# Pooled attention and a gated convolution: two blocks convolved at once without exchanged copies of h, and keys loaded and pooled by pairs of sequences

## The chip, the cores and the metric

The kernel runs on one core of a Trainium2 chip. The metric is device time in microseconds (us). The core has five engines that work side by side, each through its own queue of instructions in order: TensorE (matrix products and transposes, PE in the profile; its weight loads are listed apart as PEld), VectorE (DVE), ScalarE (ACT), GpSimd (POOL) and SyncE (SP). Data move between main memory and the on-chip memory (SBUF) by DMA; here GpSimd issues nearly all loads and SyncE nearly all stores. TensorE writes its results into eight PSUM banks, from which VectorE or ScalarE fetch them. An instruction waits until the semaphores of the work it depends on are set, and everything behind it on its engine waits with it.

## The reference

Eight sequences of 576 rows, eight heads of 64 columns. Keys and values are averaged over 8 rows each, so that 72 are left per head; the queries attend to these; the result, with the heads beside each other (512 columns), goes through a feed-forward part with a convolution of three taps along the sequence, which forms a gate.

```python
k_p = k.reshape(B, H, Sp, pool, D).mean(axis=3)      # B=8, H=8, Sp=72, pool=8, D=64
v_p = v.reshape(B, H, Sp, pool, D).mean(axis=3)
scores = scale * np.matmul(q, k_p.transpose(0, 1, 3, 2))
attn = np.exp(scores - np.max(scores, axis=-1, keepdims=True))
attn = attn / (np.sum(attn, axis=-1, keepdims=True) + 1e-09)
x = np.matmul(attn, v_p)          # then (B, S, H * D): 8 x 576 x 512
h = np.maximum(x @ w_in, 0.0)     # 512 -> 1024
conv_out = sum(conv_w[t][None, None, :] * hp[:, t:t + S, :] for t in range(3))   # hp: h, padded by a row
gate = 1.0 / (1.0 + np.exp(-conv_out))
out = h * gate @ w_out            # 1024 -> 512, float32
```

## The kernel before

**Order.** Every piece of work is an `Op` with a key (`Graph`, L34). `Graph.order` (L97) plays the program through with assumed durations and buffers and, whenever an engine comes free, takes the ready piece with the smallest key (TensorE prefers, by `STAY`, a piece of the array mode it is in). The order that this gives is the order of each engine's queue on the chip; the durations in it only choose that order. The constants (`STAY` to `URGENT`) and the table `NUDGE` (L70) shift the keys of kinds of work and of single pieces: ('l', ...) are the loads at the start, ('k', b), ('q', b), ('v', b) the preparation of a sequence, ('a', b) its attention, ('f', b) its feed-forward part, ('o', b) its output product. On-chip buffers come in rings (L300); a piece that takes a buffer waits until the last user of the one before is through. PSUM is given out by banks or pairs of neighbouring banks (`place`, L139).

**Groups.** The eight sequences go in four groups of two. A group has nine attention tiles of 128 rows (`parts`, L548): t 0 to 3 of its first sequence, t 4 half of each (the split tile), t 5 to 8 of its second; 36 in all.

**Loads and keys.** GpSimd issues the loads, which turn float32 into bfloat16 on the way. A key or query load (`load_heads`, L352) puts 576 rows of 64 for each of eight heads into four heaps of 128 partitions, 9 rows on each. Keys of sequence 0 come in two halves, queries of sequence 0 in two parts. `prep_k` (L464) pools and turns the keys on TensorE, by products with a pooling matrix `pm`; in the mode HALF these are 36 products of 144 columns on half the array, in QUARTER 72 of 72 columns on a quarter. `copy_k` (L487) brings them to `kT`. `prep_q` (L526) turns queries by transposes; `copy_q` copies them. `prep_v` (L499) sums values on VectorE in three adds (L503: 1280, 640, 320 columns) and multiplies them by a mask of heads into `vm` (L507, 960 columns; its `mask` operand is read with a step of 0 along the 64 columns).

**Attention tile.** Scores (L572 or L585), maximum on VectorE (`negm`, L598), shift on VectorE (`sd`, L610) or, in group 0, TensorE (L618), exponential on ScalarE (L636), its transpose to `eT` by TensorE and a copy (L661) in groups 0 and 1 and by a DMA of SyncE (L656) in groups 2 and 3, product with the values (L672), reciprocal and division on VectorE (L685, L687, `x<-psum,r`: "the division"), and a transpose to `xT`, by TensorE (L704) for groups 0 and 1, by a DMA (L696) after.

**Feed-forward part.** For each of the eight blocks `fb` of 128 columns of h: the input product (`ffn_in`, L717, 8 matmuls of 288 columns) and relu on ScalarE (L726). Sequence 0 has it by tiles of rows (L738, L748). The convolution (`ffn_conv`, matmuls at L803) multiplies by diagonal 64x64 matrices `dw`, one for each tap, on the four quarters of the array: two halves r of the input partitions times two halves c of the output's. Half r of the columns (288 of 576) is given to input half r, so each output half c needs both, and for r unequal to c the rows of h have to lie in the other half of the partitions. `ffn_swap` (copies at L783) makes these exchanged copies `hX`, two of 64x1152 for each pair of blocks, on VectorE or ScalarE:

```python
for n in range(max(map(len, todo))):
    for r in range(2):
        for c in range(2):
            ...
                out=cps[c * D:(c + 1) * D, r, lo:hi],
                lhsT=dw[r * D:(r + 1) * D, int(r != c), tap * n_fb + fb, :],
                rhs=hT[r * D:(r + 1) * D, fb, src:src + hi - lo] if r == c
                else hX[r * D:(r + 1) * D, fb % 2, src:src + hi - lo],
```

ScalarE takes tanh of half the sum (L815), VectorE adds 1 (L825) and multiplies by h (L826) into `gT`: "the gate". The output product (`ffn_out`, L833, eight matmuls of 512 columns a tile) needs all eight gates of the sequence, for the split tile those of both; it is copied from PSUM by VectorE or ScalarE (L844) and stored (`ffn_store`, L856) by two DMAs of 64 rows from SyncE. The last tile alone is copied in two halves of columns by both engines, and its two stores go from SyncE and from ScalarE (L1130 to L1136).

**Pieces that the change touches.** `add_load` (L904), `add_prep` (L972, keys and queries), `add_prep_v` (L1006), `add_ffn` (L1069) and `early` (L921, the loads of the start).

## Time and profile before

| | |
|---|---|
| median of 3 runs | 244.5 us (244.48 to 244.52) |
| profiled execution, span | 244.0 us |
| mean granted TensorE clock in it | 0.996 |
| TensorE busy | 220.9 us, 91% of the span |
| VectorE busy | 182.0 us, 75% |
| ScalarE busy | 168.3 us, 69% |
| GpSimd busy | 29.1 us, 12% |
| read from / written to main memory | 32.52 / 9.44 MB |

The profile is of one execution, whose span of 244.0 us runs from the first to the last instruction. Durations of instructions, and times counted from the span's start, are from it. A matmul's end is modelled and matmuls overlap, so TensorE's busy time is not a measure of how near it is to its full pace. A row of a group of instructions gives: line of the kernel, engine, operation, output<-inputs, shapes, count | busy us, mean ns of one | idle time of the engine just before them and what ended most of it. The row of busy shares in 40 slices has a digit for each 6.1 us, in tenths. Rows of a stretch begin with from:to and its length in us, then for PE, PEld, DVE, ACT, POOL the busy us and the number of instructions, the granted clock, the DMA share and GB/s. Rows of the timeline begin with the time and the duration; "ACTq" and "SPq" there are the instructions by which those engines issue a DMA.

### The profile page before, as it was taken

How to read it: one execution, taken by the hardware profiler on the slowest of the kernel's cores; microseconds unless marked ns; L12 is line 12 of the kernel's file. 1: busy time of each engine (PE TensorE's matmuls, PEld its weight loads, DVE VectorE, ACT ScalarE, POOL GpSimd, SP SyncE). 2: the span in 40 equal slices, each digit the busy share in tenths (PEclk: the TensorE clock that was granted, in tenths of full speed). 3: DMA queues.
4: the chain of work that ended last, by engine and by line, in shares of the span. 5: the costliest groups of instructions: out<-in, count | busy, mean ns of one | idle time of the engine just before them, and what ended most of it. 6: DMA issues, size and time to landing. Idle time of an engine off the chain costs nothing.

```text
span 244.0 us, 7852 instructions
## 1 busy us (share of the span) xinstructions
PE 220.9 (91%) x3354; PEld 154.3 (63%) x3377; DVE 182.0 (75%) x398; ACT 168.3 (69%) x264; POOL 29.1 (12%) x48
## 2 busy tenths in 40 slices
PE   6568998998999999999999996979999999899991
PEld 2446986876675676678775554757655576676440
DVE  7667648899999999999999995755799413956301
ACT  2254764599996876498998654949966386989330
POOL 7942223200122020220010000000000000000000
PEclk9999999999999999999999999999999999999998
DMA  5999999999189958697208568593216577400356
GB/s 81 164 205 207 207 208 208 207 207 202 22 141 185 197 83 190 104 179 153 46 3 141 126 134 91 107 139 89 24 46 149 109 137 167 117 3 6 84 137 164
DMA packets 43707, 31.53 MB, mean 129 GB/s; under 512 B 23680, under 2 KB 39064, under 8 KB 43672
## 3 DMA queue, kind: packets, MB, share of 16 engines
q0 software_dynamic: 15952, 16.26, 42.2%
q1 hardware_dynamic: 27640, 14.64, 29.5%
q8 instruction: 26, 0.43, 0.7%
q10 hardware_dynamic: 80, 0.13, 0.2%
q14 instruction: 9, 0.07, 0.1%
HBM read 32.52 MB, written 9.44 MB: 172 GB/s over the span
## 4 chain that ended last, share of the span: by engine, by line
PE 51%; DVE 26%; ACT 8%; DMA 7%; issue 5%; POOL 0%; SPq 0%; DVEq 0%; ACTq 0%; POOLq 0%
PE psum L833 16%; PE psum L717 14%; PE psum L803 7%; DVE negm L598 5%; DVE gT L826 4%; PE psum L672 3%; DVE sd L610 3%; DMA kp<-in_k_dram 3%; PE psum L738 3%; DVE tg L825 2%; ACT hT L726 2%; DVE hX L783 2%; DVE x L687 2%; DVE v L503 2%; DMA eT<-e 2%
## 5 line engine op out<-in xcount | busy, mean ns | idle before, releaser
L833 PE MATMUL psum<-w_out_sb,gT 128*128 128x512 bf16 x266 | 66.6, 379 | 2.0 <-issue 0.8
L717 PE MATMUL psum<-xT,w_in_sb 128*128 128x288 bf16 x448 | 61.1, 286 | 2.0 <-DMA xT<-x 1.3
L717 PEld LDWEIGHTS <-w_in_sb 128*128 128x128 bf16 x448 | 41.8, 98 | 15.4 <-DMA xT<-x 1.6
L833 PEld LDWEIGHTS <-gT 128*128 128x128 bf16 x288 | 26.0, 98 | 25.9 <-issue 0.7
L815 ACT ACTIVATE tg<-psum 128x576 bf16<-128x576 f32 x64 | 37.8, 655 | 3.0 <-PE psum L803 2.5
L726 ACT ACTIVATE hT<-psum 128x576 bf16<-128x576 f32 x56 | 34.4, 648 | 7.5 <-PE psum L717 7.1
L844 ACT COPY osb<-psum 128x512 f32<-128x512 f32 (+1 forms) x31 | 17.9, 579 | 24.5 <-PE psum L833 23.3
L783 DVE COPY hX<-hT 64x1152 bf16<-64x1152 bf16 x41 | 18.7, 458 | 18.3 <-ACT hT L726 15.4
L803 PE MATMUL psum<-hT,dw 64*64 64x224 bf16 (+3 forms) x576 | 30.9, 246 | 0.8 <-ACT tg L815 0.7
L803 PEld LDWEIGHTS <-dw 64*64 64x64 bf16 x1152 | 24.7, 107 | 10.5 <-issue 9.5
L826 DVE TENSOR_TENSOR gT<-tg,hT 128x576 bf16<-128x576 bf16 x64 | 29.3, 458 | 2.2
L803 PE MATMUL psum<-hX,dw 64*64 64x288 bf16 (+3 forms) x576 | 30.7, 246 | 0.0
L598 DVE TENSOR_REDUCE negm<-psum 128x8 f32<-128x576 f32 (+1 forms) x36 | 25.9, 750 | 2.4 <-PE psum L585 2.2
L783 ACT COPY hX<-hT 64x1152 bf16<-64x1152 bf16 x23 | 26.4, 1150 | 0.5
L687 DVE TENSOR_TENSOR x<-psum,r 128x512 bf16<-128x512 f32 x36 | 24.9, 692 | 1.2
L636 ACT ACTIVATE e<-sd 128x576 bf16<-128x576 f32 x27 | 18.2, 682 | 8.1 <-DVE sd L610 6.7
L672 PE MATMUL psum<-vm,eT 128*128 128x130 bf16 (+5 forms) x240 | 18.5, 222 | 4.2 <-DMA eT<-e 2.2
L825 DVE TENSOR_SCALAR tg<-tg 128x576 bf16<-128x576 bf16 x64 | 19.4, 304 | 3.4 <-ACT tg L815 3.2
L672 PEld LDWEIGHTS <-eT 128*128 128x128 bf16 (+1 forms) x240 | 14.7, 100 | 9.4 <-issue 3.0
L610 DVE TENSOR_TENSOR sd<-psum,negm 128x576 f32<-128x576 f32 x27 | 19.6, 749 | 0.1
L685 DVE RECIPROCAL r<-psum 128x8 f32<-128x8 f32 x36 | 7.3, 201 | 8.8 <-PE psum L672 8.7
L543 ACT COPY qT<-psum 128x1152 bf16<-128x1152 bf16 (+2 forms) x11 | 10.7, 992 | 4.2 <-PE psum L533 4.1
(67 smaller groups left out, 227.9 us busy)
## 6 DMA issues: line engine op xcount, KB each, us to landing
out_dram<-osb SPq DMA_DIRECT2D x71, 128.0 KB, 2.4
v<-in_v_dram POOLq DMA_DIRECT2D x8, 512.0 KB, 8.8
kp<-in_k_dram POOLq DMA_DIRECT2D x7, 576.0 KB, 16.0
qp<-in_q_dram POOLq DMA_DIRECT2D x7, 576.0 KB, 12.5
w_in_sb<-in_moe_w_in_dram POOLq DMA_DIRECT2D x2, 512.0 KB, 14.7
w_out_sb<-in_moe_w_out_dram POOLq DMA_DIRECT2D x1, 1024.0 KB, 20.0
kp<-in_k_dram POOLq DMA_DIRECT2D x2, 288.0 KB, 5.4
v<-in_v_dram POOLq DMA_DIRECT2D x8, 64.0 KB, 8.4
```

What stands on the lines that cost most here:

```text
L598: nc.vector.tensor_reduce(out=a["m"][0:rows], in_=a["s"][0:rows, :, 0:2 * KW].rearrange("p a (h s) -> p a h s", s=Sp), axis=AX.X, op=OP.ma ...
L610: nc.vector.tensor_tensor(out=a["d"][0:rows], in0=a["s"][0:rows, :, 0:2 * KW].rearrange("p a (h s) -> p a h s", s=Sp), in1=a["m"][0:rows]. ...
L672: nc.tensor.matmul(out=a["o"][lo:hi, h // 4, (h % 4) * (D + 1):(h % 4 + x1 - x0) * (D + 1)], lhsT=a["eT"][:, j, lo:hi], rhs=buf("vm", b)[: ...
L687: nc.vector.tensor_tensor(out=a["x"][0:rows].rearrange("p (a h d) -> p a h d", a=2, d=D), in0=ov[:, :, :, 0:D], in1=r[0:rows].unsqueeze(3) ...
L717: nc.tensor.matmul(out=banks(ps)[:, j, 0:SC], lhsT=w_in_block(dc, fb), rhs=buf("xT", g)[:, dc, i * S + j * SC:i * S + (j + 1) * SC], start ...
L726: nc.scalar.activation(out=buf("hT", b)[:, fb, :].rearrange("p (a s) -> p a s", a=2), in_=banks(ps)[:, :, 0:SC], func=ACT.Relu, scale=0.5,)
L783: copy(out=buf("hX", b, f2)[r * D:(r + 1) * D, :, :], in_=buf("hT", b)[(1 - r) * D:(2 - r) * D, 2 * f2:2 * f2 + 2, :],)
L803: nc.tensor.matmul(out=cps[c * D:(c + 1) * D, r, lo:hi], lhsT=dw[r * D:(r + 1) * D, int(r != c), tap * n_fb + fb, :], rhs=hT[r * D:(r + 1) ...
L815: nc.scalar.activation(out=tg.rearrange("p (a s) -> p a s", a=2), in_=banks(ps)[:, :, 0:SC], func=ACT.Tanh, scale=0.5,)
L825: nc.vector.tensor_scalar(out=tg, in0=tg, scalar1=1.0, scalar2=None, op0=OP.add)
L826: nc.vector.tensor_tensor(out=buf("gT", g)[:, fb, i * S:(i + 1) * S], in0=tg, in1=buf("hT", b)[:, fb, :], op=OP.mult)
L833: nc.tensor.matmul(out=bank(ps)[0:rows, :], lhsT=buf("gT", g)[:, fb, t * P:t * P + rows], rhs=w_out_sb[:, fb, :], start=(fb == 0), stop=(f ...
```

## The change

- The convolution takes two blocks at once (`f2`). Each input half r is multiplied for both blocks; the even block's results go to the same half of the partitions, the odd block's to the other. The two column halves go in two turns, in which the input halves change columns. No exchanged copies are made, and `dw` holds one set of matrices instead of two (two builds instead of four); the convolution weights come in one small DMA instead of two. The odd block's output so stands with its halves of partitions exchanged in PSUM and in `tg`, and its gate undoes this: instead of one add of 1 over 128 partitions there are two over 64, from one half to the other.
- The keys of sequences 2 to 7 are loaded by pairs: one DMA for two sequences, which puts nine runs of 8 rows (the rows of one pooled key, 512 values, 1 KB in bfloat16) on each of 128 partitions, in a single buffer `kk`, which is also that of sequences 0 and 1. VectorE sums them in place by three adds (2304, 1152, 576 columns); TensorE turns the sums by 18 half-array products of 64 columns with a matrix `pick` that selects and orders rows; four copies bring them to `kT`.
- The head mask is widened once to 64 columns (`mask_wide`), and the masked product reads that.
- Constants and `NUDGE` have other values, with keys of their own for pooling and turning pairs, and for the loads of queries, values and key pairs of later sequences. The order on all engines follows from these. The planner gains `two_pairs`, for a piece that takes two pairs of banks.

The change is described as also issuing all stores from SyncE; the diff has no line for that. The diff, cut (of `NUDGE`, single lines):

```diff
-    STAY = 111.55
-    LAZY = 1.11
+    STAY = 2454.96
+    LAZY = 7.6
...
-        ('l', 'ident'): -61.73, ('l', 'k0'): -86.22, ('l', 'k0+'): -94.89, ('l', 'k1'): 2.95, ('l', 'k2'): 53.08, ('l', 'k3'): 66.15,
-        ('l', 'mask'): -87.39, ('l', 'out'): 38.13, ('l', 'pm'): 4.15, ('l', 'q0'): -15.29, ('l', 'q0+'): 17.25, ('l', 'q1'): 12.42,
+        ('kk', 1): 7482.77, ('kk', 2): -20886.29, ('kk', 3): -46.32, ('l', 'ident'): 33950.61, ('l', 'k0'): -19474.68, ('l', 'k0+'): 335.78,
+        ('l', 'k1'): 12294.96, ('l', 'kk1'): -19285.24, ('l', 'mask'): -6614.65, ('l', 'out'): 15911.81, ('l', 'pm'): 22677.96, ('l', 'q0'): -5102.49,
+        ('l', 'q0+'): -18723.75, ('l', 'q1'): -16061.86, ('l', 'q2'): -15420.86, ('l', 'q3'): -1573.38, ('l', 'v0'): 10274.77, ('l', 'v1'): 20982.95,
+        ('l', 'v2'): -1384.76, ('l', 'w0'): 12979.54, ('l', 'w1'): -5970.38, ('lk', 4): -9398.62, ('lk', 6): -10401.99, ('lq', 4): -8677.67,
...
-                f = place(need)
+                f = place(need) if need <= 2 else two_pairs()
...
+        def two_pairs():
+            f = [idle_from(x) for x in banks]
+            c = sorted(max(now, f[i], f[i + 1]) for i in range(0, len(f), 2) if None not in (f[i], f[i + 1]))
+            return c[1:2] or None
...
-             "hT": 2, "gT": 2, "xT": 2, "qT": 3, "kp": 3, "qp": 2, "hX": 3, "v": 2, "vm": 5, "kT": 5, "sd": 3, "r": 3, "s": 2}
+             "hT": 2, "gT": 2, "xT": 2, "qT": 3, "kk": 1, "qp": 2, "v": 2, "vm": 5, "kT": 5, "sd": 3, "r": 3, "s": 2}
...
+    mask_wide = const.tile([P, NJ, 3, D], BF16, name="mask_wide")
+    pick = const.tile([P, 2, D], BF16, name="pick")
...
-    cw_raw = const.tile([3 * n_fb, 3 * D], FP32, name="cw_raw")
-    convw = const.tile([P, 2, 3 * n_fb], FP32, name="convw")
+    cw_raw = const.tile([3 * n_fb, P], FP32, name="cw_raw")
+    convw = const.tile([P, 3 * n_fb], FP32, name="convw")
     ident_2 = const.tile([P, D], BF16, name="ident_2")
-    dw = const.tile([P, 2, 3 * n_fb, D], BF16, name="dw")
+    dw = const.tile([P, 3 * n_fb, D], BF16, name="dw")
...
+    def load_pair(g):
+        rows = k[groups[g][0]:groups[g][1] + 1].rearrange("b h s d -> (b h s) d").rearrange("(p r) d -> p (r d)", p=P)
+        nc.gpsimd.dma_start(out=buf("kk", g)[:, :, 0:POOL * D], in_=rows.rearrange("p (c x) -> p c x", c=C))
...
-        nc.sync.dma_start(out=cw_raw[:, 0:P], in_=cw)
-        nc.sync.dma_start(out=cw_raw[:, P:P + D], in_=cw[:, 0:D])
+        nc.sync.dma_start(out=cw_raw, in_=cw)
...
+    def widen_mask():
+        nc.vector.tensor_copy(out=mask_wide, in_=mask.unsqueeze(3).to_broadcast([P, NJ, 3, D]))
+
+    def build_pick():
+        for hh in range(2):
+            for f in range(2):
+                nc.vector.tensor_copy(
+                    out=pick[:, hh].rearrange("p (s f a e) -> p s f a e", s=2, f=2, a=2)[:, :, f],
+                    in_=ident.rearrange("p (s a hh f e) -> p s a hh f e", s=2, a=2, hh=2, f=2)[:, :, :, hh, f],
+                )
...
-        x, n = (part - 1) // 2, 3 * n_fb // 2
-        todo = slice((part - 1) % 2 * n, (part - 1) % 2 * n + n)
+        n = 3 * n_fb // 2
+        todo = slice((part - 1) * n, part * n)
         nc.vector.tensor_tensor(
-            out=dw[:, x, todo],
+            out=dw[:, todo],
             in0=ident_2.unsqueeze(1).to_broadcast([P, n, D]),
-            in1=convw[:, x, todo].unsqueeze(2).to_broadcast([P, n, D]),
+            in1=convw[:, todo].unsqueeze(2).to_broadcast([P, n, D]),
             op=OP.mult,
...
+    def pool_pair(g, step):
+        t, half = buf("kk", g), POOL * D >> step + 1
+        nc.vector.tensor_tensor(out=t[:, :, 0:half], in0=t[:, :, 0:half], in1=t[:, :, half:2 * half], op=OP.add)
+
+    def turn_pair(g, ps):
+        flat = banks(ps).rearrange("p a x -> p (a x)")
+        for c in range(C):
+            for hh in range(2):
+                nc.tensor.matmul(
+                    out=flat[hh * D:(hh + 1) * D, c * D:(c + 1) * D],
+                    lhsT=buf("kk", g)[:, c, 0:D],
+                    rhs=pick[:, hh],
+                    start=True,
+                    stop=True,
+                    skip_group_check=True,
+                )
+
+    def copy_pair(b, ps, hh, copy):
+        g, i = where[b]
+        part = slice(hh * D, (hh + 1) * D)
+        src = banks(ps).rearrange("p a x -> p (a x)")[part, 0:C * D].rearrange("p (c s j e) -> p s j e c", s=2, j=4, e=8)
+        copy(
+            out=buf("kT", b)[part, :, hh * Sp:(hh + 1) * Sp].rearrange("p j (e c) -> p j e c", c=C),
+            in_=src[:, i],
...
-            in1=mask.unsqueeze(3).to_broadcast([P, NJ, 3, D]),
+            in1=mask_wide,
...
-    def ffn_swap(b, f2, r, copy):
-        copy(
-            out=buf("hX", b, f2)[r * D:(r + 1) * D, :, :],
-            in_=buf("hT", b)[(1 - r) * D:(2 - r) * D, 2 * f2:2 * f2 + 2, :],
-        )
-
-    def ffn_conv(b, fb, ps):
+    def ffn_conv(b, f2, pss):
         g, i = where[b]
-        hT, hX = buf("hT", b), buf("hX", b, fb // 2)
-        cps = banks(ps)
+        hT = buf("hT", b)
         todo = [[], []]
         for tap in (1, 0, 2):
             for lo, hi, src in conv_runs(i, tap - 1):
                 j = lo // SC
                 todo[j].append((tap, lo - j * SC, hi - j * SC, src))
-        for n in range(max(map(len, todo))):
-            for r in range(2):
-                for c in range(2):
-                    if n >= len(todo[r]):
+        for turn in range(2):
+            for n in range(max(map(len, todo))):
+                for r in range(2):
+                    j = r ^ turn
+                    if n >= len(todo[j]):
                         continue
-                    tap, lo, hi, src = todo[r][n]
-                    nc.tensor.matmul(
-                        out=cps[c * D:(c + 1) * D, r, lo:hi],
-                        lhsT=dw[r * D:(r + 1) * D, int(r != c), tap * n_fb + fb, :],
-                        rhs=hT[r * D:(r + 1) * D, fb, src:src + hi - lo] if r == c
-                        else hX[r * D:(r + 1) * D, fb % 2, src:src + hi - lo],
-                        start=(n == 0),
-                        stop=(n == len(todo[r]) - 1),
-                        skip_group_check=True,
-                    )
+                    tap, lo, hi, src = todo[j][n]
+                    for c in range(2):
+                        fb = 2 * f2 + (r ^ c)
+                        nc.tensor.matmul(
+                            out=banks(pss[r ^ c])[c * D:(c + 1) * D, j, lo:hi],
+                            lhsT=dw[r * D:(r + 1) * D, tap * n_fb + fb, :],
+                            rhs=hT[r * D:(r + 1) * D, fb, src:src + hi - lo],
+                            start=(n == 0),
+                            stop=(n == len(todo[j]) - 1),
+                            skip_group_check=True,
+                        )
...
-        nc.vector.tensor_scalar(out=tg, in0=tg, scalar1=1.0, scalar2=None, op0=OP.add)
-        nc.vector.tensor_tensor(
-            out=buf("gT", g)[:, fb, i * S:(i + 1) * S], in0=tg, in1=buf("hT", b)[:, fb, :], op=OP.mult
-        )
+        tg, gate = buf("tg", b, fb), buf("gT", g)[:, fb, i * S:(i + 1) * S]
+        if fb % 2:
+            for r in range(2):
+                nc.vector.tensor_scalar(
+                    out=gate[r * D:(r + 1) * D], in0=tg[(1 - r) * D:(2 - r) * D], scalar1=1.0, scalar2=None, op0=OP.add
+                )
+            tg = gate
+        else:
+            nc.vector.tensor_scalar(out=tg, in0=tg, scalar1=1.0, scalar2=None, op0=OP.add)
+        nc.vector.tensor_tensor(out=gate, in0=tg, in1=buf("hT", b)[:, fb, :], op=OP.mult)
...
+    def add_load_pair(g, key):
+        kk[g] = token("kk", g)
+        loads["kk", g] = add({"POOL": 0.65}, key, lambda: load_pair(g), uses=[kk[g]], land=(LATE, 2 * kb, RATE))
+
+    picked = add({"DVE": 0.5}, START + Graph.DW - 1, build_pick, after=[c0])
...
+    def add_pair(g, key):
+        b0 = groups[g][0]
+        prev = None
+        for step, d in enumerate((1.352, 0.752, 0.452)):
+            prev = add(dve(d), key + nudge("kk", g) + Graph.KPOOL + step, lambda step=step: pool_pair(g, step),
+                       after=[prev, loads["kk", g]], uses=[kk[g]])
+        t = token("ps", n=2)
+        for b in groups[g]:
+            ktok[b], kdone[b] = token("kT", b), []
+        o = add({"PE": 0.30}, key + nudge("kk", g) + Graph.KTURN, lambda: turn_pair(g, t), after=[prev, picked],
+                uses=[t, kk[g]], mode=HALF, count=36)
+        for b in groups[g]:
+            for hh in range(2):
+                c = add(either(0.46, 0.42), key + nudge("kk", g) + Graph.KTURN + 1, None, after=[o, zk], uses=[t, ktok[b]])
+                c.emit = lambda c=c, b=b, hh=hh: copy_pair(b, t, hh, copier(c))
+                kdone[b].append(c)
...
-        for step, d in enumerate((0.81, 0.49, 0.32, 1.16)):
+        for step, d in enumerate((0.81, 0.49, 0.32, 0.65)):
...
-            cb, tg = token("ps", n=2), token("tg", b, fb)
-            if fb % 2 == 0:
...
+        for f2 in range(n_fb // 2):
+            fbs = (2 * f2, 2 * f2 + 1)
+            cbs, tgs = [token("ps", n=2) for _ in fbs], [token("tg", b, fb) for fb in fbs]
+            conv = add({"PE": 0.66}, w + 6 * f2 + Graph.QCONV, lambda f2=f2, cbs=cbs: ffn_conv(b, f2, cbs),
+                       after=relu[fbs[0]] + relu[fbs[1]] + dwo, uses=cbs + tgs + [htok[b], gtok[g]], mode=QUARTER, count=64 + 12 * i)
+            for fb, cb, tg in zip(fbs, cbs, tgs):
+                o = add(act(0.65), w + 3 * fb + Graph.CONV, lambda fb=fb, cb=cb: ffn_tanh(b, fb, cb), after=[conv], uses=[tg, cb])
+                gdone.setdefault(b, []).append(
+                    add(dve(0.307, *[0.307] * (fb % 2), 0.458), w + 3 * fb + Graph.GATE, lambda fb=fb: ffn_gate(b, fb), after=[o],
+                        uses=[tg, htok[b], gtok[g]]))
```

## The prediction

> **What bounds the kernel now.** I read the page first (busy shares and slices), then the busy time of each engine by stretches cut at the events that the order of the work gives, then the groups by line and shape, and last the timeline of the start and the end. The shares and the slices of VectorE:
>
> ```profile
> PE 220.9 (91%) x3354; PEld 154.3 (63%) x3377; DVE 182.0 (75%) x398; ACT 168.3 (69%) x264; POOL 29.1 (12%) x48
> DVE  7667648899999999999999995755799413956301
> ```
>
> The stretches are cut at the first convolution (51.7), the first matmul of sequence 2's and of sequence 4's input product (about 102 and 145.9) and the last convolution (225.9); each row gives length, then busy time of PE, PEld, DVE, ACT and POOL:
>
> ```profile
> 45.60:51.70 6.10, 5.73 (x102) 4.84 (x97) 5.75 (x11) 4.17 (x8) 1.48 (x2) 1.00 1.23 206
> 51.70:99.20 47.50, 45.01 (x847) 32.35 (x853) 46.16 (x98) 38.96 (x63) 4.82 (x7) 1.00 0.83 149
> 99.20:145.90 46.70, 45.81 (x668) 31.72 (x672) 44.77 (x94) 37.61 (x58) 3.40 (x5) 1.00 0.64 110
> 145.90:159.00 13.10, 10.92 (x145) 8.16 (x144) 8.76 (x19) 9.08 (x15) 0.00 (x0) 1.00 0.69 104
> 190.00:225.90 35.90, 34.69 (x481) 24.06 (x485) 18.09 (x45) 27.92 (x42) 0.00 (x0) 1.00 0.43 90
> ```
>
> From 51.7 to 145.9 VectorE works 90.9 of 94.2 us. TensorE shows 90.8 there, but its records overlap. I therefore count columns in the order in which the built programs' instructions stand (half-array matmuls count half, quarter-array ones a quarter) and take the pace of an unbroken run:
>
> ```profile
> 102.49 5.64 PE L717 MATMUL psum<-xT,w_in_sb 128*128 128x288 bf16 x44
> 225.85 13.12 PE L833 MATMUL psum<-w_out_sb,gT 128*128 128x512 bf16 x58
> ```
>
> The first is 0.445 ns a column; the second, which is 60 matmuls in the order, 0.427. I use 0.43. The kernel has 465 thousand columns, 200 us. Up to its 26th division (x<-psum,r of the 26th of 36 attention tiles, at 145.1) it has 263.5 thousand, 113 us; from there to the last matmul at 239.0, 202 thousand, 87 us of 94. So there are three regimes: a start ruled by loads and latencies, a middle in which VectorE is full and TensorE has slack, and from about 146 on TensorE.
>
> The Trainium skill (Perfetto Trace Analysis, Identifying the Most-Contended Engine) also holds that matmul busy time is no measure of headroom and points to weight-load time: PEld's 32.35 of 47.5 agrees. Were TensorE's 45.01 of 47.5 taken as its load, only its own saved columns would count in the middle (rival B's opposite).
>
> **The change part by part.** The rows that price it:
>
> ```profile
> L783 DVE COPY hX<-hT 64x1152 bf16<-64x1152 bf16 x41 | 18.7, 458 | 18.3 <-ACT hT L726 15.4 <-PE psum L803 2.0
> L783 ACT COPY hX<-hT 64x1152 bf16<-64x1152 bf16 x23 | 26.4, 1150 | 0.5
> L825 DVE TENSOR_SCALAR tg<-tg 128x576 bf16<-128x576 bf16 x64 | 19.4, 304 | 3.4 <-ACT tg L815 3.2
> L507 DVE TENSOR_TENSOR vm<-v,mask 128x960 bf16<-128x960 bf16 x8 | 9.2, 1156 | 0.2
> L503 DVE TENSOR_TENSOR v<-v 128x1280 bf16<-128x1280 bf16 x8 | 6.5, 818 | 0.2 <-DMA v<-in_v_dram 0.2
> L503 DVE TENSOR_TENSOR v<-v 128x640 bf16<-128x640 bf16 x8 | 3.9, 489 | 0.2
> ```
>
> *Exchanged copies of h.* 41 copies on VectorE (18.7) and 23 on ScalarE (26.4) go. For them every odd block's add of 1 becomes two half-partition ones: 64 instead of 32. A 64-row instruction that crosses partition halves is the copy of h: 458 ns for 1152 columns. The add takes 304 for 576 without crossing, so I take 304 each, +9.7. Bounds: 240 (half the copy plus nothing) to 458, which is 7.7 to 19.6 in all.
>
> *Keys.* Three pairs are summed by three adds of 2304, 1152 and 576 columns. The two v rows give 0.16 us + 0.514 ns a column: 1.34 + 0.75 + 0.45 = 2.55, three times 7.6. TensorE's key columns fall from 16.9 to 5.6 thousand (180 half-array of 144 and 216 quarter-array of 72, to 36, 72 and 54 half-array of 64): 4.8 us. Query turns chosen otherwise save 0.7, two more fills cost 0.4; in all 5.3.
>
> *Widened mask.* The masked copy of v has 960 columns; with an operand that advances it should run as the adds do: 0.65 for 1.156, eight times -4.0 (bounds 0 and -4.0). The widening, once, is 0.65 to 1.16, and lies in the idle start.
>
> *Moved by the order.* Six eT copies go from VectorE to ScalarE (-2.9, +4.2 there), two of the four weight builds go (-1.9), kT copies +2.0, selectors +0.4, and two shifts come after the 26th division instead of before it (-1.5).
>
> Up to the 26th division VectorE's work thus changes by -10.0 (22 copies of h) +4.9 (16 odd blocks) +7.6 -4.0 -1.9 -2.9 +2.0 -1.5 and +0.9 of small ones: -4.9. ScalarE loses 23 copies and takes some 6 us back; it is 82% busy in the middle and its loss is hidden, but not needed.
>
> *The start.* Here the order changes most. GpSimd now issues k0 (half), q0 (second part), all of q1, half of w_in, then q0 (first part), k0 (other half), and the pooling matrix and identity come after ten loads. Loads land in the order of issue; in the timeline k0's halves landed by 8.8 and first scores ran at
>
> ```profile
> 12.25 0.42 PE L585 MATMUL psum<-kT,qT 128*128 128x144 bf16 x2
> ...
> 20.54 0.41 PE L585 MATMUL psum<-kT,qT 128*128 128x144 bf16 x4
> ```
>
> Now 2.2 MB (written) must land first, 1.66 MB more than k0; at the 205 GB/s of 10 to 20 us that is 8 us: k0 complete at about 16.5, first scores at 18 to 19, 6 late. But all four tiles of sequence 0 then run on end, where tiles 2 and 3 waited until 20.5 for q0's second part: their divisions end at 28, not 27. From there the same eight groups of the first product (1.06 each), shifts and turns follow, without the key work and score tile of group 1 (4 us): first convolution at 47.3, against 51.7, first gate at 48.9 (bounds 46 and 54).
>
> *The middle.* VectorE's rows from the first gate to the 26th division sum to 97.2; from its 9th division (45.3) to its 26th the old kernel had 104.5 rows in 99.8 us, 0.957. So 48.9 + 93.0 = 141.9 against 145.1: -3.2. That VectorE's total falls by 4.9 and the division comes only 3.2 earlier is the idle time before the first gate.
>
> *Waits added.* The keys have one buffer: a pair's load on GpSimd waits until the pair before is turned, and behind it in GpSimd's queue stand loads of v and q. Pair 1 lands at about 48 (up to its end 8.0 MB beyond k0's bytes are written: 39 us at 205 GB/s from 8.8 on) and is summed at about 56; the third load is issued at about 83, lands at 91 to 93 (8 us, the median v load takes 8.8), and is summed at about 95. Only 2 to 4 us of cover; beyond them each us is lost, with VectorE's in-order queue (gates) behind it. TensorE's turn waits for the sums with query turns behind it. A convolution waits for two relus and two pairs of banks; the next input product queues behind it. The copy of h (0.46 to 1.15) that stood between relu and convolution is gone, so I cost this at nothing; an uncovered 0.2 a pair would be 6.4.
>
> *The end.* After the 26th division TensorE has 199.7 thousand columns left against 202: 85.9 against 86.8, -0.9, with the same 7 us of stalls (the eT and xT transposes wait in SyncE's queue before and after alike). The last tile's rows:
>
> ```profile
> 238.66 0.37 ACT L844 COPY osb<-psum 128x256 f32<-128x256 f32 x1 [0.75 <-DVE osb L844]
> 239.06 0.59 ACTq L856 DMA_DIRECT2D out_dram<-osb  x1
> 239.06 0.69 DVE L844 COPY osb<-psum 128x512 f32<-128x512 f32 x1 [0.44 <-ACT osb L844]
> ```
>
> The split tile (two halves one after the other, then two stores at once) now comes last instead of last but one: 0.42 + 0.37 for 0.69 in copies, but one store issue instead of two (0.8): -0.7. The diff changes nothing else in the stores: the last half still goes from ScalarE. On SyncE one of two small weight loads goes, at the start, hidden.
>
> **Sum.** -3.2 - 0.9 - 0.7 = -4.8 on the span of 244.0; the median of the runs shown, 244.5, is 0.5 above that span, so 239.7.
>
> **The rivals.**
> A, VectorE's middle does not shorten: crossing adds at 458 (16 by then two each, +4.9) or an unimproved mask product (+4.0). It gives 243.7 to 244.6. For it: no row has a crossing add. Against: the crossing copy runs at 0.4 ns a column.
> B, the reverse of taking TensorE as full: freed of the middle's copies, it also runs ahead with output products, so less than 200 thousand columns stand behind VectorE. If half of the middle's saved key work (5 thousand columns, 2 us) and the 2.2 and 1.3 us waits for eT and xT go, 234 to 237. For it: 16 us of slack in the middle. Against: output products need the last gates.
> C, slower: the start. If the 6 us delay of the first scores passes through undiminished, the first gate comes at 54 or later; from 53.9 on (5.0 later than I take) all is lost, at 55 to 57 the time is 246 to 248. For it: q1 and w_in, needed late, go ahead of k0. Against: tiles 2 and 3, and sequence 1, waited for other loads anyway.
> D, slower: the paired convolution. Its two row halves swap banks halfway, and may meet in one bank; if one drains first, that is a matmul of 0.29 in each of 32 pairs, up to 9.3: 244 to 249, slower from 0.15 a pair on. No row shows two halves in one bank. The Trainium skill (TensorEngine Tiling, Gotcha 1: PSUM Pressure) says that row tiles cannot access one bank at the same time; no run here shows it.
>
> **How the numbers follow.** Main forecast 0.46 (237 to 242.5), B 0.18, A 0.15 (a quarter of it within 0.2%, which is about what a measurement tells from no change), C 0.11, D 0.05, others slower 0.05. Faster: 0.46 + 0.18 + 0.11 = 0.75; same 0.04; slower 0.21. The range 234.5 to 246 leaves out the best of B and the worst of C and D, about 0.2. The main case alone is 237 to 242.5.
>
> **What would show it.** No hX rows; 64 half adds near 304 ns; sums of keys near 1.34, 0.75, 0.45; masked copies near 0.65; first scores at 18 to 19, first convolution near 47; VectorE full from 49 to 142; 26th division at 142; last matmul at 235. The forecast falls if VectorE waits for a pair's load before a key sum, if TensorE waits at the convolutions' start, or if the first gate comes after 52.

## The result, and the profile after

The changed kernel takes 247.51 us (median of four runs, 246.54 to 248.62) against 244.49 for the kernel before (243.91 to 244.52): a ratio of 1.0124, with a 95% interval of 1.0075 to 1.0174. It is 3.0 us slower; 239.7 (234.5 to 246.0) was forecast. Ratios here and below leave disturbed executions out, so that one may differ a little from the quotient of two medians.

The profiled execution has a span of 246.9 us, 2.9 more than the one of before. Its busy shares, VectorE's slices and the granted TensorE clock by slices (tenths):

```profile
PE 218.5 (89%) x3206; PEld 149.4 (61%) x3206; DVE 175.9 (71%) x397; ACT 149.1 (60%) x245; POOL 27.9 (11%) x45
...
DVE  7278757999999989789999992466689701965200
...
PEclk9779999999999999999999998899999999999998
```

Every engine works less than before (VectorE 6.1 us, ScalarE 19.2), and the kernel is longer. VectorE's first slices have a 2 where TensorE waits for its first work, its full stretch now has gaps, and the clock falls twice, which before it did only in the last slice.

Times of the same events in the two profiles, each the start of the first such instruction in the timeline (the last matmul: its end), and what had been forecast for them:

| us | before | forecast | after |
|---|---|---|---|
| first scores | 12.2 | 18 to 19 | 18.3 |
| 4th division (end) | 27.3 | 28 | 28.5 |
| first convolution | 51.7 | 47.3 | 47.1 |
| first gate (its product) | 54.6 | 48.9 | 49.1 |
| 9th division | 45.3 | | 46.0 |
| 18th division | 100.9 | | 97.7 |
| 26th division | 145.1 | 141.9 | 145.1 |
| last matmul | 239.0 | 234.9 | 242.1 |
| span | 244.0 | 239.2 | 246.9 |

Up to the 18th division the changed kernel is as far ahead as forecast. By the 26th it has lost that, and behind it another 3.1.

The rows of VectorE that answer to those shown of before:

```profile
L867 DVE TENSOR_SCALAR gT<-tg 64x576 bf16<-64x576 bf16 x64 | 20.0, 313 | 1.2
L552 DVE TENSOR_TENSOR vm<-v,mask_wide 128x960 bf16<-128x960 bf16 x8 | 5.2, 654 | 0.2
L520 DVE TENSOR_TENSOR kk<-kk 128x2304 bf16<-128x2304 bf16 x3 | 4.1, 1354 | 0.7 <-DMA kk<-in_k_dram 0.7
L520 DVE TENSOR_TENSOR kk<-kk 128x1152 bf16<-128x1152 bf16 x3 | 2.2, 750 | 0.0
L520 DVE TENSOR_TENSOR kk<-kk 128x576 bf16<-128x576 bf16 x3 | 1.4, 450 | 0.0
```

The prices were right: 304 and 0.65 and 1.34, 0.75, 0.45 had been taken. Busy time of VectorE up to the 26th division is 124.2 us after and 127.8 before, 3.6 less; its idle time up to there is 20.9 and 17.3, 3.6 more. (The sum of its durations, where overlapping instructions count in full, fell by 3.9; 4.9 had been forecast.) So no kind of instruction costs clearly more than forecast; the waits are what is new. VectorE's, from the 97th us on (engine, line, what it waited for: us, times, longest):

```profile
DVE v L548 <- DMA v<-in_v_dram: 1.2, 1, 1.2
DVE kk L520 <- DMA kk<-in_k_dram: 0.7, 1, 0.7
DVE kT L539 <- ACT kT L539: 0.5, 1, 0.5
```

Before, none of its waits between 46 and 146 for a load was over 0.2. And then the place just behind the 26th division. Timeline of the changed kernel:

```profile
141.07 4.86 SPq L741 DMA_TRANSPOSE xT<-x  x3
...
141.20 0.76 POOL L365 DMA_DIRECT2D qp<-in_q_dram  x1 [40.62 <-PE psum L578]
...
146.10 1.30 SPq L701 DMA_TRANSPOSE eT<-e  x1
...
152.86 0.83 PE L717 MATMUL psum<-vm,eT 128*128 128x130 bf16 x6 [4.38 <-DMA eT<-e]
```

GpSimd's last load, the queries of sequence 7 (576 KB), has waited 40.62 us for its buffer, which the turn of sequence 6's queries frees at about 141. It goes out in the same microsecond as three transposes of x and lands at 150.54. In the stretch from 140 to 153 the DMA view (issues, KB each, median us to landing) gives, after:

```profile
qp<-in_q_dram POOLq DMA_DIRECT2D x1, 576.0 KB, 9.3
...
xT<-x SPq DMA_TRANSPOSE x4, 6.8
```

and before, where no load runs there (that of the same queries went out at 126.83 and had landed at 134.15):

```profile
xT<-x SPq DMA_TRANSPOSE x5, 2.5
```

SyncE issues one transpose behind the other, the eT that the values of a tile need came late, and TensorE waited 4.38 us instead of 2.18. In the six microseconds after that its clock was down (from:to and length, busy us of PE, PEld, DVE, ACT, POOL, granted clock, DMA share, GB/s), after:

```profile
152.00:158.00 6.00, 5.14 (x37) 3.89 (x38) 1.63 (x4) 1.64 (x3) 0.00 (x0) 0.72 0.65 129
```

and before, with the wait of 2.18 as the list of waits has it:

```profile
PE psum L672 <- DMA eT<-e: 2.2, 1, 2.2
```

```profile
152.00:158.00 6.00, 6.00 (x95) 4.70 (x96) 4.36 (x11) 5.89 (x9) 0.00 (x0) 1.00 0.50 100
```

At 0.72, six microseconds do 4.3 us of work. The wait (+2.2) and the clock (+1.7), less the 0.9 us of columns saved as forecast, make 3.0 of the 3.1 us lost behind the 26th division. The Trainium skill (TensorE: Matmul & The Clock Gate, Part 1) says that the clock halves after an idle window of about 3.4 us. The trace agrees: it stayed at 1.00 behind the wait of 2.18 and fell behind that of 4.38.

### The profile page after: what moved, and what is told of

Same layout as the page of the kernel before. It is cut to its first block, busy times and chain, and to the rows that moved or that the text cites. A ratio compares the mean times of both kernels' runs of the same rounds, so it can differ in the third digit from the quotient of the medians.

```text
span 246.9 us, 7525 instructions
## 1 busy us (share of the span) xinstructions
PE 218.5 (89%) x3206; PEld 149.4 (61%) x3206; DVE 175.9 (71%) x397; ACT 149.1 (60%) x245; POOL 27.9 (11%) x45
## 4 chain that ended last, share of the span: by engine, by line
PE 39%; DVE 32%; DMA 16%; ACT 5%; issue 5%; POOL 2%; DVEq 0%; ACTq 0%; POOLq 0%
PE psum L878 11%; PE psum L762 11%; DVE gT L873 6%; DMA eT<-e 6%; DVE negm L643 5%; PE psum L844 5%; DVE gT L867 4%; DMA qp<-in_q_dram 4%; DMA v<-in_v_dram 4%; DVE sd L655 4%; DVE x L732 3%; PE psum L783 3%; PE psum L717 3%; DVE v L548 3%; ACT tg L855 2%
## 5 line engine op out<-in xcount | busy, mean ns | idle before, releaser
L878 PE MATMUL psum<-w_out_sb,gT 128*128 128x512 bf16 x288 | 69.6, 379 | 0.3 <-ACT tg L855 0.2
L762 PE MATMUL psum<-xT,w_in_sb 128*128 128x288 bf16 x448 | 62.8, 290 | 0.7 <-ACT tg L855 0.6
L844 PE MATMUL psum<-hT,dw 64*64 64x288 bf16 (+4 forms) x1152 | 30.2, 246 | 0.0
L889 ACT COPY osb<-psum 128x512 f32<-128x512 f32 (+1 forms) x34 | 19.7, 580 | 16.6 <-PE psum L878 14.2
L867 DVE TENSOR_SCALAR gT<-tg 64x576 bf16<-64x576 bf16 x64 | 20.0, 313 | 1.2
L872 DVE TENSOR_SCALAR tg<-tg 128x576 bf16<-128x576 bf16 x32 | 9.8, 306 | 10.8 <-ACT tg L855 10.8
L630 PE MATMUL psum<-kT,qT 128*128 128x144 bf16 (+1 forms) x136 | 12.8, 226 | 3.8 <-DVE kT L539 1.3
L873 DVE TENSOR_TENSOR gT<-tg,hT 128x576 bf16<-128x576 bf16 x32 | 14.7, 458 | 1.1
L873 DVE TENSOR_TENSOR gT<-gT,hT 128x576 bf16<-128x576 bf16 x32 | 14.6, 458 | 1.1
L630 PEld LDWEIGHTS <-qT 128*128 128x128 bf16 (+1 forms) x136 | 9.3, 98 | 7.8 <-issue 5.1
```

The source lines that it names most:

```text
L630: nc.tensor.matmul(out=heads[lo:hi, f], lhsT=buf("qT", b)[:, f, a, t % 5 * P:t % 5 * P + hi - lo], rhs=buf("kT", b)[:, 2 * f + a, :], star ...
L762: nc.tensor.matmul(out=banks(ps)[:, j, 0:SC], lhsT=w_in_block(dc, fb), rhs=buf("xT", g)[:, dc, i * S + j * SC:i * S + (j + 1) * SC], start ...
L844: nc.tensor.matmul(out=banks(pss[r ^ c])[c * D:(c + 1) * D, j, lo:hi], lhsT=dw[r * D:(r + 1) * D, tap * n_fb + fb, :], rhs=hT[r * D:(r + 1 ...
L867: nc.vector.tensor_scalar(out=gate[r * D:(r + 1) * D], in0=tg[(1 - r) * D:(2 - r) * D], scalar1=1.0, scalar2=None, op0=OP.add)
L873: nc.vector.tensor_tensor(out=gate, in0=tg, in1=buf("hT", b)[:, fb, :], op=OP.mult)
L878: nc.tensor.matmul(out=bank(ps)[0:rows, :], lhsT=buf("gT", g)[:, fb, t * P:t * P + rows], rhs=w_out_sb[:, fb, :], start=(fb == 0), stop=(f ...
```

## Experiments

Theory after this reading: (1) the load of queries that runs beside the transposes costs some 4 us; (2) late loads in the middle cost some 2; (3) VectorE bounds the middle, so that what the change takes off it is worth its length. Rivals: to (1), that the transposes hold each other up or that the queries themselves are late; to (3), that another engine is right behind; and a fourth question, whether the later start passes through to the end.

Most of these kernels keep the order of all queues exactly. An extra buffer is given to one load, or single instructions are moved in the finished order or cut short. "Base" below is the changed kernel with two loads made early (it stands under "Late loads in the middle"). All ratios are to the kernel before, run beside it. Distances are from the profiles, of one execution each: from the 9th to the 26th division (the middle) and from there to the last matmul (the end).

| kernel | median us | ratio, 95% | first gate | middle | end |
|---|---|---|---|---|---|
| before | 244.5 | 1 | 54.6 | 99.8 | 93.9 |
| changed | 247.5 | 1.0124 (1.0075, 1.0174) | 49.1 | 99.1 | 97.0 |
| changed, queries 7 early | 244.1 | 0.9963 (0.9929, 0.9998) | 51.1 | 99.1 | 92.5 |
| the same, load in the wrong place | 244.9 | 0.9986 (0.9949, 1.0022) | 48.9 | 99.4 | 92.7 |
| the same, load in the old place | 246.8 | 1.0089 (1.0047, 1.0131) | 49.6 | 98.8 | 96.0 |
| before, load added late | 250.5 | 1.0230 (1.0173, 1.0288) | 54.6 | 99.9 | 99.1 |
| base: queries 7, last keys early | 243.0 | 0.9918 (0.9879, 0.9958) | 50.8 | 96.8 | 93.1 |
| base, no key sums | 242.4 | 0.9906 (0.9870, 0.9943) | 51.8 | 95.7 | 92.2 |
| base, no half adds | 242.5 | 0.9829 (0.9728, 0.9929) | 52.1 | 95.6 | 92.5 |
| base, half of an output product | 244.0 | 0.9972 (0.9935, 1.0009) | 49.1 | 96.7 | 93.8 |
| base, that and no key sums | 242.4 | 0.9886 (0.9813, 0.9958) | 51.4 | 94.2 | 92.9 |
| before, wide mask | 242.5 | 0.9906 (0.9872, 0.9941) | 53.0 | 98.2 | 93.6 |
| before, copies cut | 241.2 | 0.9864 (0.9802, 0.9926) | 53.1 | 97.7 | 92.6 |
| base, identity early | 244.4 | 0.9980 (0.9947, 1.0012) | 51.5 | 96.7 | 92.6 |
| base, keys first | 243.5 | 0.9931 (0.9892, 0.9970) | 50.8 | 96.8 | 92.4 |
| base, keys first, turn later | 241.0 | 0.9845 (0.9793, 0.9896) | 48.0 | 96.8 | 92.4 |

### One load beside the transposes

The queries of sequence 7 get a buffer of their own, the order stays:

```diff
+    while len(buffers["qp"]) <= 2:
+        buffers["qp"].append(const.tile(*shapes["qp"], name=f"qp{len(buffers['qp'])}"))
...
+    todo = graph.order()
+    tokens["qp", 7].slots = [2]
     with tc.manual_schedule():
-        for o in graph.order():
+        for o in todo:
```

> The changed kernel in its own order; only the queries of sequence 7 get a third buffer, so that their load no longer waits until the queries of sequence 5 are turned (139.7 us). Theory 1, collision: that load (issued at 141.20, landed at 150.54) runs beside the transposes of x and e that SyncE issues from 141.07 on, and makes them land 5 to 9 us after issue instead of 1.4 to 2.5. Then it is now issued at about 101, the transposes issued from 141 to 148 land within 3 us, TensorE's wait of 4.38 us before 152.86 falls to 2.2 or less, the granted clock stays at 1.00 in 152 to 158, and the time falls by 3 to 4.5 us, to 243 to 244.5. Theory 2, SyncE's own queue: the transposes hold each other up (the kernel before also waits 2.18 us there, with its load at 126.8 to 134.2): no change, 247.5 within 0.7.

Measured: 244.1 us, ratio 0.9963. The load went out at 102.58 and landed at 112.27, the median landing of xT in 140 to 153 fell from 6.8 to 3.3 us, TensorE's wait there from 4.4 to 0.3, the clock stayed at 1.00, and the end took 92.5 us instead of 97.0 (93.0 had been forecast):

```profile
PE psum L719 <- DMA eT<-e: 0.3, 1, 0.3
```

```profile
152.00:158.00 6.00, 5.85 (x93) 4.38 (x91) 3.22 (x8) 3.64 (x6) 0.00 (x0) 1.00 0.60 116
```

The loss behind the 26th division is explained by this one load. That leaves whether it is the load's traffic or the queries coming late, so a load that nobody reads was put back:

```diff
+    at = todo.index(loads["q", 7][0])
+    spare = buffers["qp"][tokens["qp", 5].slots[0]]
+    todo.insert(at + 1, Op({}, 0, lambda: load_heads(spare, q, 7), (), None, None, 0))
```

> As the run with the early load, and at the old place a second load of the same 576 KB into the buffer that the queries of sequence 5 leave, which nobody reads. Theory 1: the transposes are slow again and the time returns to 247 to 248, though no instruction needs the load. Theory 2, or a theory in which the late queries themselves are what is waited for: the time stays where the run with the early load has it, within 0.7 us.

Measured: 244.9, 0.9986. This missed its place: the buffer chosen was that of sequence 5, free earlier, so that the load ran from 128.10 to 135.47, between two chains of transposes (none is issued from 124 to 134). It shows only that a load there does no harm that can be told (the end took 92.7 us against 92.5). With the buffer of sequence 6 (`tokens["qp", 6]`), whose turn the changed kernel's load had waited for:

> The second load in the earlier run went out at 128.10 and had landed by 135.47, before the transposes, since it waited for the queries of sequence 5; those whose turn ends at about 140 are sequence 6's. So here: the changed kernel, the queries of sequence 7 loaded early into a third buffer, and an unread load of 576 KB into the buffer of sequence 6, behind that turn, where the changed kernel had its load. Collision: it is issued at 140 to 143, transposes issued in the next 6 us land 5 us or more after issue, TensorE waits 3 us or more once between 146 and 154, the clock falls below 0.9 there, and the time is 2.5 to 4.5 us above the run with the early load (244.1), 246.5 to 248.5. Rival, the late queries themselves were waited for: time within 0.8 us of 244.1.

Measured: 246.8, 1.0089, and the lines of the changed kernel come back: TensorE's longest wait, and its clock behind it.

```profile
PE psum L719 <- DMA eT<-e: 3.6, 1, 3.6
```

```profile
152.00:158.00 6.00, 5.73 (x43) 4.41 (x44) 1.80 (x4) 1.95 (x3) 0.00 (x0) 0.72 0.53 106
```

Nobody reads what this load brings, so the cause is the load being under way there, and not queries that come late. Where the two meet (DMA engines, memory, a queue) was not taken apart. Last, such a load added to the kernel before, held back by a memory set on GpSimd that waits for a small VectorE copy behind the 24th division:

```diff
+    x24 = ...                       # the 24th division, 141.2 us
+    def late_load():
+        nc.vector.memset(flag, 0.0)
+        nc.vector.tensor_copy(out=flag[:, 1:2], in_=flag[:, 0:1])
+        nc.gpsimd.memset(flag[:, 0:1], 0.0)
+        load_heads(buffers["qp"][tokens["qp", 6].slots[0]], q, 7)
+    todo.insert(todo.index(x24) + 1, Op({}, 0, late_load, (), None, None, 0))
```

> The kernel before, its order kept, with one unread load of 576 KB more, issued by GpSimd after the 24th division (about 141.5 us), where the changed kernel had its last load of queries. Collision: the transposes of x and e that SyncE issues in the 7 us behind it land 4 us or more after issue instead of 1.2 to 2.5, TensorE's wait before 150.8 grows from 2.2 to 4 or more, and the kernel before becomes 2 to 4.5 us slower (ratio 1.008 to 1.018), about what the changed kernel is. Rival, the collision hurts only the changed kernel's order: ratio within 0.004 of 1.

Measured: 250.5, 1.0230, more than expected. The load ran from 143.12 to 151.12, the transposes of x had a median landing of 6.6 us and those of e 4.8, TensorE waited 5.9 us and its clock was 0.50 in 152 to 158:

```profile
PE psum L673 <- DMA eT<-e: 5.9, 1, 5.9
```

```profile
152.00:158.00 6.00, 3.40 (x18) 2.40 (x19) 1.35 (x3) 1.54 (x2) 0.00 (x0) 0.50 0.69 97
```

So this is a property of the place and not of the changed operations: the same added bytes cost 0.8 us at 128, within the intervals (second kernel of this part), 2.7 at 142 (third) and 6 at 143 in the kernel before. The three small instructions that hold the load back there were not run without it.

### Late loads in the middle

The last pair of keys gets a second buffer of 9.4 KB a partition, besides the third of the queries:

```diff
+    while len(buffers["kk"]) <= 1:
+        buffers["kk"].append(const.tile(*shapes["kk"], name=f"kk{len(buffers['kk'])}"))
...
+    tokens["qp", 7].slots = [2]
+    tokens["kk", 3].slots = [1]
```

> As the run with the early load, and the last pair of keys has a buffer of its own, so that its load (issued at 89.97, landed at 100.89) goes out at about 71. Theory, late loads in the middle: VectorE's waits of 0.67 us for this pair (before 100.91) and of 1.2 for the values of sequence 6 (before 105.28, their load ran beside the keys') go; the 26th division comes at 142.5 to 143.5 instead of 145.1, and the time is 1 to 2.5 us under the run with the early load. Rival: the values land as late as before, since their buffer is free only at 94.7; then only the 0.67 goes and the gain is under 0.7.

Measured: 243.0, 0.9918. The load went out at 72.34 and had landed by 89.34; the values of sequence 6 landed at 102.25 instead of 105.18, and both waits of VectorE for loads are gone. The middle fell from 99.1 to 96.8, 2.3 us, as the theory had it. The 26th division came at 144.5 and not at 142.5 to 143.5, since this execution began 1.7 us later than the changed kernel's; the times differ by 1.1, within their intervals.

### What bounds the middle

One small part of the change alone, in the kernel before: the masked products read the widened mask.

```diff
-            in1=mask.unsqueeze(3).to_broadcast([P, NJ, 3, D]),
+            in1=mask_wide,
...
+        nc.vector.tensor_copy(out=mask_wide, in_=mask.unsqueeze(3).to_broadcast([P, NJ, 3, D]))
```

> The kernel before in its own order, with the mask widened once and the masked products of the values read from it: one small part of the change alone. Theory, VectorE bounds the middle: each of eight products takes 0.65 instead of 1.16; six lie between the first gate and the 26th division, which comes at 142 instead of 145.1, and the time falls by 2 to 3 us, to 241.5 to 242.5. Rival, the middle is held by something else (TensorE, loads, the transposes): the rows get shorter and the time stays within 0.7 us of 244.5.

Measured: 242.5, 0.9906, with products of 656 ns for 1156. VectorE's 4 us were worth 2.3 in time, and the 26th division came at 142.0, 3.1 earlier. Half of that (1.6) was there at the 9th division, in an execution whose first scores came 0.9 earlier; the middle became 1.6 shorter for 2.9 us less of VectorE's durations in it. So VectorE bounds the middle of the old kernel, but only in part, and this one part of the change gives, alone and with nothing else moved, about half of what had been forecast for the whole change. Then the copies of h, cut short in the kernel before (its `hX` buffers are cleared once at the start, since most of them is not written any more):

```diff
-            out=buf("hX", b, f2)[r * D:(r + 1) * D, :, :],
-            in_=buf("hT", b)[(1 - r) * D:(2 - r) * D, 2 * f2:2 * f2 + 2, :],
+            out=buf("hX", b, f2)[r * D:(r + 1) * D, :, 0:16],
+            in_=buf("hT", b)[(1 - r) * D:(2 - r) * D, 2 * f2:2 * f2 + 2, 0:16],
```

> The kernel before, its order kept, with the exchanged copies of h cut from 576 to 16 columns a block: most of h is not exchanged and nothing is put in the copies' place. 22 copies on VectorE (10.1 us, perhaps 8 saved) lie before the 26th division, and 26.4 us of ScalarE's go. Theory, VectorE bounds the middle until TensorE does: 26th division at 137 to 140 instead of 145.1, time 237.5 to 240 against 245.0. Rival, ScalarE or TensorE holds the middle as much: 26th division after 142 and the time above 242.

Measured: 241.2, 0.9864. The copies fell from 458 to 169 ns on VectorE and from 1150 to 215 on ScalarE: 6.3 us off VectorE in the middle, 21.5 off ScalarE in the whole kernel, and nothing put in their place. The middle became 2.1 us shorter, not 6. It lies between the two theories: twice the work taken off gave little more than the mask alone. What holds the rest, the base can tell, which has the mask's gain already. First the key sums, then the second of the half adds:

```diff
-        nc.vector.tensor_tensor(out=t[:, :, 0:half], in0=t[:, :, 0:half], in1=t[:, :, half:2 * half], op=OP.add)
+        nc.vector.tensor_tensor(out=t[:, :, 0:8], in0=t[:, :, 0:8], in1=t[:, :, half:half + 8], op=OP.add)
```

> The run with both early loads (242.99), its order kept, with the nine sums of keys cut to 8 columns a row: the sums of the keys of sequences 2 to 7 are left out. It takes some 6.5 of the 7.7 us of key sums off VectorE, all before the 26th division. Theory, VectorE bounds the middle and each microsecond moved onto it there counts: the 26th division comes 5 to 6.5 us earlier in its distance from the first gate (93.7 us in that run) and the time falls by 3.5 to 6 us, to 237 to 239.5. Rival, another engine is right behind: less than 2 us.

```diff
-            for r in range(2):
-                nc.vector.tensor_scalar(
-                    out=gate[r * D:(r + 1) * D], in0=tg[(1 - r) * D:(2 - r) * D], scalar1=1.0, scalar2=None, op0=OP.add
-                )
+            nc.vector.tensor_scalar(out=gate, in0=tg, scalar1=1.0, scalar2=None, op0=OP.add)
```

> The run with both early loads (242.99), its order kept, with one add of 1 over 128 partitions for an odd block instead of two over 64 that cross: the exchange of the halves is left undone. It takes 32 times 0.31 us off VectorE, 16 of them (4.9 us) before the 26th division. Theory, VectorE bounds the middle: the distance from the first gate to the 26th division falls from 93.7 by 4 to 5 us and the time by 2.5 to 4.5 us, to 238.5 to 240.5. Rival, another engine is right behind: less than 1.5 us.

Measured: 0.9906 and 0.9829. (The second rests on two executions, of 239.8 and 241.0 us; its interval is 0.02 wide, and its profile is of another one, of 244.0.) The middle shrank by 1.1 and 1.2 us, where 6.0 (nine sums of 187 ns instead of 7.7 us) and 4.9 us of work had gone. The theory that each microsecond on VectorE counts falls; the rival, another engine right behind, was tested on TensorE, by leaving out every second matmul of the first group's output product:

```diff
-        for fb in range(n_fb // 2 * j, n_fb // 2 * (j + 1)):
+        n = 2 if g == 0 else 1
+        for fb in range(n_fb // 2 * j, n_fb // 2 * (j + 1), n):
...
-                stop=(fb == n_fb - 1),
+                stop=(fb == n_fb - n),
```

> The run with both early loads (242.99), its order kept, with every second of the eight matmuls left out of the output products of sequences 0 and 1: half of their sum is missing. It takes 36 matmuls of 512 columns off TensorE, 7.8 us at the 216 ns from one to the next, between 66 and 125. Taking 6.5 us off VectorE there had given only 0.5 us. Theory, TensorE bounds the middle as soon as VectorE is relieved a little: the 26th division comes 4 us or more earlier in its distance from the first gate (93.7) and the time falls by 3 to 6 us, to 237 to 240. Rival, neither engine alone but the fixed order of several queues and the latencies between them: less than 2 us, 241 to 243.5.

> Both cuts together, order kept: half of the output products of sequences 0 and 1 and the key sums of sequences 2 to 7 are left out (7.8 us of TensorE, 6.5 of VectorE). Theory, two engines close to each other: each cut alone gives little, both together 5 us or more, 236 to 238. Theory TensorE alone: like the output cut alone within 1 us. Theory, order and latencies: still less than 3 us, above 240.

Measured: 0.9972 and 0.9886 against 0.9918 for the base. TensorE's 7.8 us alone shorten the middle by 0.1; both cuts, 13.8 us of work, by 2.6. That is more than the two alone (1.2), so the engines hold each other up a little, and far from the 5 or more that two full engines side by side would give. In the chain of waits of the last of these kernels a block of input products stands beside many pieces of 0.3 to 1.2 us that change engines:

```profile
99.95 3.67 PE psum L766 x30
103.62 0.90 PE psum L848 x24
...
104.54 1.19 ACT tg L859 x2
...
105.76 0.40 ACT kT L543
...
106.19 0.45 DVE kT L543
...
106.89 0.46 DVE gT L877
...
107.59 0.34 issue
107.93 0.75 DVE negm L647
```

Convolution, tanh, key copies, gate, maximum: a fixed order of several queues, in which an engine that is faster only waits longer for the one before it. That this is the limit was not shown by a run of its own (ScalarE's work was not cut in the base, where it is busy 73% of the stretch from the first gate to the 26th division, and the number of PSUM banks can't be raised). Shown is that neither VectorE's nor TensorE's amount of work alone is the limit.

### The start

In the changed kernel the first query turn waits for the identity matrix, which GpSimd builds after ten loads (11.71 us, the queries having landed at 7.86); TensorE is idle and its clock falls:

```profile
6.00:12.00 6.00, 0.70 (x9) 0.40 (x9) 1.35 (x6) 0.30 (x1) 5.86 (x10) 0.76 1.17 173
12.00:18.00 6.00, 5.57 (x109) 4.57 (x105) 4.60 (x11) 2.89 (x5) 2.58 (x4) 0.68 1.28 204
```

First scores came at 18.1 to 21.1 in the nine kernels with this start, and what follows is shifted with them: 20.3 and 18.3 in the first experiment and in the changed kernel, then 29.7 and 27.8 (4th division), 51.1 and 49.1 (gate), 147.1 and 145.1 (26th division). Three kernels move this in the finished order of the base. The first has the identity behind the second load in GpSimd's queue, and the pooling matrix behind the third:

```diff
+    put([identity], q0b)       # take out of the order, and put behind this
+    put([pool_m], q1l)
```

> The run with both early loads (242.99); in GpSimd's queue alone the identity is built after the first two loads and the pooling matrix after the third, instead of after ten loads. In the changed kernel the first query turn waited for the identity until 11.71 (12.45 in that run), 4 us after its queries had landed, TensorE stood idle from 6 and the granted clock was 0.50 from 10 to 15 or 18. Theory, the start passes through to the end and part of it is this wait: the first turn comes at 8 to 9, the first scores at 17 to 18 (18.3 to 21.1 so far), the time falls by 0.5 to 2 us, to 241 to 242.5. Rival, the second half of the keys (landed at 16.4) sets the start anyway: no change within 0.5.

```diff
+    put([identity, k0b, q0a, head_m, pool_m, v0l, q1l], q0b)
...
+    put([p_q1[0]], maxes[2])    # the turn of sequence 1's queries, in banks 6 and 7
+    put([c_q1[0]], p_q1[0])
+    put([p_q1[1]], maxes[3])
...
+    put([c_q1[1], later], p_q1[1])
+    put([picked] + dwo, vdone[0])
```

> As the run with the early identity, and in GpSimd's queue the second half of the keys and the other part of the queries of sequence 0, then its values, go ahead of the queries of sequence 1 and of w_in; the turn of sequence 1's queries and the two weight builds stand behind the scores of sequence 0 instead of ahead. Theory, the start's delay passes through to the end: first scores at 13 to 15, fourth division at 23 to 25 instead of 27.8 to 30, first gate at 47 to 48.5, and the time 2 to 4 us under the run with both early loads, 239 to 241. Rival, what comes between (w_in, the product by tiles, later loads) absorbs it: first gate and 26th division within 1 us of before, time within 0.8 us of 243.

Measured: 0.9980 and 0.9931; neither is better than the base. With the identity early the first turns began before 9, but the scores still came at 20.6, since they wait for the second half of the keys (landed at 17.1), and the clock was down again behind the next idle stretch. With the keys first the scores came at 13.7, but the fourth score tile stood behind the turn of sequence 1's queries, which had been moved to landing at 18.0; the first product by tiles began at 29.6 (base 30.0) and the first gate came at the same 50.8. Here the expectation missed because a moved load made a new wait. Then that turn was moved behind the first transpose of x, and the two weight builds behind the copies of sequence 1's keys:

```diff
-    put([p_q1[0]], maxes[2])
...
-    put([p_q1[1]], maxes[3])
...
+    put(p_q1, turn1)            # banks 6, 7 and 4, 5
...
-    put([picked] + dwo, vdone[0])
+    put([picked] + dwo, kdone[1][-1])
```

> The run with keys first had its scores at 13.7 but the turn of sequence 1's queries, placed between the third and the fourth score tile, waited for its load (landed at 18.0), and the first product by tiles began at 29.6 as before. Here that turn stands behind the first transpose of x, and the two weight builds behind the copies of sequence 1's keys. In all runs so far the first gate follows that product's start by 20.2 to 21.2 us. Theory, the start passes through: the fourth division comes at 23 to 26, the product starts at 25.5 to 27.5 (w_in has landed at 25.4), the first gate at 46.5 to 48.5, and the time is 1.5 to 4 us under the run with both early loads (ratio to the kernel before 0.976 to 0.986). Rival, the later work (loads of group 1, order of the queues) absorbs it: the first gate moves, the 26th division stays after 143.5, the ratio stays at 0.989 to 0.995.

Measured: 241.0, 0.9845. 4th division at 25.7, first product at 25.95, first gate at 48.0 (base 50.8), 26th division at 141.8 (144.5), span 239.3 (242.7). The first product began 4.1 us earlier than in the base and the first gate 2.8 us; the middle is the base's and the end 0.7 shorter, so in these two executions the 2.8 us pass through to the end. By the medians the gain over the base is 2.0 us: the base's profile is of an execution 1.4 us above its median, this one of the median itself. The lines of the start:

```profile
13.75 0.66 PE L634 MATMUL psum<-kT,qT 128*128 128x144 bf16 x8 [0.70 <-DVE kT L517]
...
25.95 1.07 PE L787 MATMUL psum<-xT,w_in_sb 128*128 128x128 bf16 x16
```

The rival, that later work absorbs a better start, falls: the first experiment's start, 2.0 us later than the changed kernel's in the same order, had come through whole as well (147.1 for 145.1). Nothing is left out of this kernel; it is 1.6% (1.0 to 2.1) faster than the kernel before, where the changed one is 1.2% slower.

## Why the prediction was wrong, point by point

*The prices and the start: right.* First scores 18.3 (18 to 19), 4th division ended at 28.5 (28), first convolution 47.1 (47.3), first gate 49.1 (48.9). That the first gate met the forecast to 0.2 is in part luck: in the nine kernels with this start it came at 48.9 to 52.1. Half adds of 313 ns (304 was taken, 458 the bound), masked products of 0.654, key sums as above. What was missing there is that the start had still more to give: the first gate is set by when the first product begins, and that by loads and by an identity matrix far back in GpSimd's queue.

*The middle, -3.2: measured 0.0.* VectorE's durations from the first gate to the 26th division sum to 97.4 us (97.2 forecast), but they took 96.0 us and not 93.0. The failing step is the pace of 0.957 taken from the kernel before (99.8 over 104.5 is 0.955); it was 0.986. VectorE was idle for 6.6 us of the middle instead of 3.6, because of new waits: 1.2 us for values (0.2 before), 0.7 for the last pair of keys (none), 1.1 for key copies on ScalarE (0.2). The part on waits added had named the second: "Only 2 to 4 us of cover; beyond them each us is lost", and still the sum had nothing for it. The last pair's load was put at 83, landing at 91 to 93; it went out at 89.97 and landed at 100.89; why the pair before it was turned so late, no run asks. With that load early the distance from the first gate to the 26th division is 93.7, against 93.0 forecast.

*The end, -0.9: measured +3.1.* The failing step is "with the same 7 us of stalls (the eT and xT transposes wait in SyncE's queue before and after alike)". The transposes stood in the queue alike, but one load had moved beside them. The prediction has the order of the loads in GpSimd's queue; what the DMA engines carry at the time when a load will go out it did not ask. The profile of before held the price: the four transposes issued from 101.35 to 105.95, beside loads of values that landed by 107.34, landed after 4.8 to 7.8 us, and the two of 114.92 and 116.46, with no load beside them, after 2.6 and 2.5. With the load out of the way the end took 92.5 us, against 93.0 forecast.

*The tail, -0.7: measured -0.2* (from the last matmul to the end of the span 4.8 us, 5.0 before); why it is not more, no run shows.

*What is left.* With both loads early the profiled execution has a span of 242.7 us, 3.5 above the 239.2 forecast: 1.9 in the start, which scatters, 0.7 in the middle, 0.1 in the end and 0.8 in the tail.

*VectorE bounds the middle: right in part.* The forecast took every microsecond off VectorE as won until TensorE's columns set the end. In the kernel before, 2.9 us off it in the middle (the wide mask) gave 1.6 there and 6.3 (the copies) 2.1; in the base 6.0 or 4.9 us more gave 1.1 and 1.2. The sentence that TensorE has slack in the middle was right: in the base it is busy 94% from the first gate to the 26th division, and 7.8 us less of it gave 0.1. So was the page of the Trainium skill cited there (Perfetto Trace Analysis, Identifying the Most-Contended Engine), by which matmul busy time is no measure of headroom. But it does not follow that the other busy engine is the bound all the way.

*The rivals.* A (half adds or masks dear) falls by its prices. B (TensorE runs ahead) did not come. C, as it was put, fell: the first gate came at 49.1 and not at 54; its kernel of truth, that the start passes through to the end, was shown by the last kernel with the keys first. D (the paired convolution loses in PSUM) falls: from the first weight load of a pair of blocks to the next other instruction it takes 0.87 us for 32 matmuls and 0.88 for 40, in both kernels (medians). The Trainium skill's rule on row tiles in one bank (TensorEngine Tiling, Gotcha 1: PSUM Pressure) therefore cost nothing here; whether two ever met in one bank, no run shows. What happened, a load that meets transposes, was none of the rivals.
